# Program order, hand-dealt PSUM banks, one run of value products and idle products in an attention and mixer kernel

## The chip, the cores and the metric

The kernel runs on one core of a Trainium2 chip. The metric is the time of one execution in microseconds (us), median of several. Every number here is from a run of the original kernel ("before"), of the changed one ("after") or of one of twelve experiments. The kernel before scatters by about 1% from run to run, the changed ones by about 0.5%; a few runs of the kernel before counted as slow (883.67 us below is one) and are left out of every ratio.

## The reference

Two steps. First a thresholded attention over 8 batches, 8 heads, 576 positions and head size 64; of each row of scores only those within `tau` of the row's maximum are kept. Its output is then the input of a mixer: a low rank term over the positions and two dense layers.

```python
scores = scale * np.matmul(q, k.transpose(0, 1, 3, 2))
thresh = np.max(scores, axis=-1, keepdims=True) - tau
scores = np.where(scores >= thresh, scores, -1e9)
attn = np.exp(scores - max);  attn = attn / (sum + 1e-9)        # cut
x = np.matmul(attn, v)                                          # heads side by side: (8, 576, 512)
h = x.transpose(0, 2, 1) @ U @ V                                # rank 32
u = x + h.transpose(0, 2, 1)
out = u + np.maximum(u @ w_ch1, 0.0) @ w_ch2                    # 512 -> 2048 -> 512
```

## The kernel before

It goes through 32 pairs of heads (8 batches of 4), each in five row tiles: four of 128 rows, and a fifth with the last 64 rows of both heads. One step of the program is one row tile. Three pairs are in flight: the scores of pair p, the value products of p-1, and what follows them for p-2. The mixer of a finished batch is cut into units, put in beside the next batch's attention.

For a tile of scores, each head j uses its own half of the array's rows (partitions 0 to 63 or 64 to 127). VectorE then empties the PSUM and finds the row's extreme (`s_sb`), ScalarE exponentiates (`e_sb`), VectorE selects and sums (`w_ring`, `den`), and a DMA transposes the weights (`wT`).

```python
psS = pool("psS", 2, PSUM)      # two score tiles of two banks
ps1 = pool("ps1", 4, PSUM)      # four single banks for all else
...
sct = [psS.tile([P, 2, 512], FP32, name="sc", tag="sc") for _ in range(2)]
for c in range(2):
    for j in range(2):
        hs = slice(64 * j, 64 * j + 64)
        nc.tensor.matmul(sct[j][:, c, 0:HC], self.qT[hs, i * P:(i + 1) * P],
                         self.kT[hs, c * HC:(c + 1) * HC], start=True, stop=True)
```

In the fifth tile the second head's row sums lie in the other half of the partitions, so a tiny DMA moves them; the reciprocal of the sums reads it in the step in which the value products end:

```python
            if i == 4:
                if self.b % 2 == 0:
                    nc.sync.dma_start(self.den[0:HB, 4, 1:2], self.den[HB:P, 4, 0:1])
                ...                       # odd batches: two such copies
    def evacuate(self):                   # called at step 4 of the next pair
        ...
            nc.vector.tensor_scalar(out=self.rec[part, ts, :], in0=self.den[part, ts, :],
                                    scalar1=1e-9, scalar2=None, op0=ALU.add)
            nc.vector.reciprocal(out=self.rec[part, ts, :], in_=self.rec[part, ts, :])
```

The program states this order, but a scheduler of the framework decides the order in which each engine gets its instructions, and the pools decide which bank a tile gets. The scheduler takes this reciprocal early, almost a pair before its place in the program: in the stretch that the prediction shows, the copies were issued at 406.75 and 409.18 us, and VectorE stood at the reciprocal until 410.91.

## Time and profile before

| kernel before | |
|---|---|
| time, median of the first 3 runs | 874.38 us (867.46 to 883.67) |
| span of the profiled run | 869.7 us |
| mean granted TensorE clock | 0.931 (no record before 53.9 us; the views count that as 1.00) |
| start, until the first tile's end mark | 13.8 us |
| pairs 0 to 4, before the mixer has work | 106.7 us |
| 27 pairs with the mixer beside them | 690.8 us, 25.6 each |
| tail: the last batch's mixer | 58.4 us |

The stretches are cut at the last two transposes of a pair, the end of its attention weights. They are used the same way for each kernel below, so that "the middle" is always the same work: 27 pairs. The lines of the page, the stretches and the waits stand in the prediction. One line that it did not use belongs to the argument later. It is a row of the costliest groups: busy time, mean ns of one, then the engine's idle time just ahead of the group and what ended it.

```profile
L203 PE MATMUL sc<-qkT 64*128 64x288 f32 x1024 | 245.9, 477 | 21.6 <-DVE s_sb L219 21.1
```

These are the score products of the first four tiles, three tenths of all the time for which TensorE counts as busy (245.9 of 810.0 us).

### The profile page before, as it was taken

What the parts mean: (1) busy time and instruction counts of PE and PEld (TensorE: products, weight loads), DVE (VectorE), ACT (ScalarE), POOL (GpSimd) and SP (SyncE); (2) the same over time, 40 slices, a digit from 0 to 9 for tenths busy, and PEclk for the clock granted to TensorE, in tenths of its full rate; (3) what the DMA queues carried; (4) which work ended last, traced back from release to release, by engine and by line L of the source; (5) the groups of instructions that cost most, each with busy time, mean ns of one, the idle gap of its engine ahead of it and who ended that gap; (6) DMA issues with size and microseconds to landing.
All of it is one profiled execution on the core that took longest, in us unless ns stands there. A gap on an engine that the chain in (4) does not pass through costs nothing.

```text
span 869.7 us, 15087 instructions
## 1 busy us (share of the span) xinstructions
PE 810.0 (93%) x5064; PEld 458.3 (53%) x5064; DVE 532.1 (61%) x1548; ACT 446.8 (51%) x1089; POOL 310.7 (36%) x469
## 2 busy tenths in 40 slices
PE   5998899989999999989999999898999999999997
PEld 3554555534565556544566445553456545655473
DVE  3768686546766776456675577544676577746401
ACT  3545556624676447543476345653457644755260
POOL 9675655324443333243342444403443233000000
PEclk9998889968999999878899799996899999989989
DMA  6999988446654656444665478534567576424302
GB/s 124 149 163 169 154 140 117 86 86 119 129 103 81 123 123 112 84 99 84 108 109 96 106 120 125 103 50 103 118 105 98 87 119 129 82 46 73 69 1 61
DMA packets 225309, 90.29 MB, mean 104 GB/s; under 512 B 208512, under 2 KB 213568, under 8 KB 225232
## 3 DMA queue, kind: packets, MB, share of 16 engines
q1 hardware_dynamic: 205376, 56.98, 41.1%
q0 software_dynamic: 18640, 32.06, 18.7%
q8 instruction: 40, 0.66, 0.3%
q10 hardware_dynamic: 1216, 0.30, 0.2%
q14 instruction: 37, 0.30, 0.1%
HBM read 36.86 MB, written 9.44 MB: 53 GB/s over the span
## 4 chain that ended last, share of the span: by engine, by line
PE 56%; DVE 10%; DMA 9%; ACT 6%; SPq 5%; issue 2%; ACTq 0%; DVEq 0%
PE sc L203 13%; PE ch L370 13%; PE p L347 11%; DMA den<-den 9%; PE av L260 6%; DVE s_sb L219 5%; SPq L242 5%; ACT e_sb L226 5%; PE sc L211 4%; DVE w_ring L234 3%; PE ups L321 2%; PE qkps L146 2%; PE tps L311 2%; PE ch L373 1%; PE ups L323 1%
## 5 line engine op out<-in xcount | busy, mean ns | idle before, releaser
L226 ACT ACTIVATE e_sb<-s_sb,m 128x576 bf16<-128x576 f32 x288 | 216.1, 774 | 240.4 <-DVE s_sb L219 234.6
L219 DVE TENSOR_SCALAR_CACHE_REDUCE s_sb<-sc 128x576 f32<-128x576 f32 x288 | 209.5, 753 | 179.3 <-PE sc L203 143.9
L203 PE MATMUL sc<-qkT 64*128 64x288 f32 x1024 | 245.9, 477 | 21.6 <-DVE s_sb L219 21.1
L234 DVE SCALAR_TENSOR_TENSOR w_ring<-s_sb,thr,e_sb 128x576 bf16<-128x576 f32 x288 | 229.7, 820 | 38.0 <-ACT e_sb L226 29.1
L135 POOL TENSOR_TENSOR vh<-vraw,vh 128x512 bf16<-128x512 f32 x64 | 52.7, 841 | 397.9 <-ACT vh L134 355.0
L203 PEld LDWEIGHTS sc<-qkT 64*128 64x128 f32 x1024 | 129.1, 205 | 89.6 <-DVE s_sb L219 35.7
L347 PE MATMUL p<-uT,W1b 128*128 128x288 bf16 x1024 | 151.1, 295 | 5.6 <-ACT Rb L351 5.0
L370 PE MATMUL ch<-W2b,Rb 128*128 128x512 bf16 x512 | 134.8, 408 | 0.9 <-ACT uT L324 0.9
L260 PE MATMUL av<-wT,vh 128*64 128x288 bf16 (+1 forms) x1280 | 128.6, 310 | 1.4 <-DMA wT<-w_ring 1.3
L347 PEld LDWEIGHTS <-W1b 128*128 128x128 bf16 x1024 | 96.4, 100 | 60.9 <-issue 36.9
L260 PEld LDWEIGHTS <-vh 128*64 128x64 bf16 (+1 forms) x1280 | 76.7, 115 | 32.8 <-issue 19.3
L370 PEld LDWEIGHTS <-Rb 128*128 128x128 bf16 x512 | 49.0, 103 | 64.7 <-issue 24.2
L351 ACT ACTIVATE Rb<-p 128x288 bf16<-128x288 f32 x128 | 52.1, 407 | 23.9 <-PE p L347 23.5
L380 DVE TENSOR_TENSOR o<-ch,x 128x512 f32<-128x512 f32 x36 | 24.5, 680 | 61.5 <-PE ch L373 58.1
L355 ACT ACTIVATE Rb<-p 128x224 bf16<-128x224 f32 x128 | 45.9, 359 | 21.4 <-PE p L347 18.5
L211 PE MATMUL sc<-qkT 64*64 64x288 f32 x256 | 51.6, 453 | 0.5 <-DVE s_sb L219 0.5
L95 POOL DMA_DIRECT2D qraw<-in_q_dram x62 | 42.5, 686 | 23.5 <-PE qkps L146 22.5
L95 POOL DMA_DIRECT2D vraw<-in_v_dram x64 | 44.1, 690 | 12.4 <-POOL vh L135 6.2
L269 ACT COPY xT<-av 128x288 f32<-128x288 f32 x64 | 22.5, 402 | 49.4 <-PE av L260 39.4
L95 POOL DMA_DIRECT2D kraw<-in_k_dram x62 | 43.0, 694 | 9.3 <-PE qkps L146 8.8
L146 PE MATMUL qkps<-ident,kraw 128*128 128x128 f32 (+1 forms) x160 | 30.0, 298 | 15.1 <-ACT qkT L150 15.1
L96 POOL DMA_DIRECT2D vraw<-in_v_dram x64 | 41.1, 642 | 1.0 <-issue 0.6
(61 smaller groups left out, 674.2 us busy)
## 6 DMA issues: line engine op xcount, KB each, us to landing
out_dram<-o SPq DMA_DIRECT2D x72, 128.0 KB, 2.4
vraw<-in_v_dram POOLq DMA_DIRECT2D x64, 80.0 KB, 2.7
wT<-w_ring SPq DMA_TRANSPOSE x320, 3.4
qraw<-in_q_dram POOLq DMA_DIRECT2D x62, 80.0 KB, 3.4
kraw<-in_k_dram POOLq DMA_DIRECT2D x62, 80.0 KB, 4.0
vraw<-in_v_dram POOLq DMA_DIRECT2D x64, 64.0 KB, 2.9
qraw<-in_q_dram POOLq DMA_DIRECT2D x62, 64.0 KB, 3.4
kraw<-in_k_dram POOLq DMA_DIRECT2D x62, 64.0 KB, 4.1
```

Of the source, the lines that this page charges most:

```text
L95: engine.dma_start(raw[0:HB, :, j, :], sv[:, 0:NT, j, :])
L135: nc.gpsimd.tensor_tensor(out=vh[0:part, ts, 1, :, :], in0=src, in1=hi, op=ALU.subtract)
L146: nc.tensor.transpose(ps[:, n:n + rows(t)], raw[0:rows(t), t, :, :], ident[0:rows(t), 0:rows(t)])
L203: nc.tensor.matmul(sct[j][:, c, 0:HC], self.qT[hs, i * P:(i + 1) * P], self.kT[hs, c * HC:(c + 1) * HC], start=True, stop=True)
L211: nc.tensor.matmul(one[hs, c, 0:HC], self.qT[hs, 512:S], self.kT[hs, c * HC:(c + 1) * HC], start=True, stop=True)
L219: nc.vector.tensor_scalar(out=s_sb.rearrange("p (a c) -> p a c", a=2), in0=sct[x][:, :, 0:HC], scalar1=0.0, scalar2=None, op0=ALU.add, op1 ...
L226: nc.scalar.activation(out=e_sb, in_=ssb[x], func=ACT.Exp, bias=m[:, x:x + 1], scale=-1.0)
L234: nc.vector.scalar_tensor_tensor(out=w_sb[:, 0:S], in0=ssb[x], scalar=thr[:, x:x + 1], in1=esb[x], op0=ALU.is_le, op1=ALU.mult, accum_out= ...
L260: nc.tensor.matmul(self.av[c][64 * j:64 * j + 64, 0:HC], self.vh[0:nk, kt, part, j, :], self.wT[0:nk, kt, j, c * HC:(c + 1) * HC], start=( ...
L347: nc.tensor.matmul(ps[:, 0:HC], W1b[:, dt, ft * P:(ft + 1) * P], bt.uT[:, dt, c * HC:(c + 1) * HC], start=(dt == 0), stop=(dt == 3))
L351: nc.scalar.activation(out=bt.Rb[:, ft, 0:HC], in_=ps[:, 0:HC], func=ACT.Relu)
L370: nc.tensor.matmul(ch, lhsT, W2b[:, ft, :], start=(ft == 0), stop=False)
```

## The change

The intent: take the order of instructions out of the scheduler's hands, so that each engine finds its work in the order in which it becomes ready, and hand out the PSUM banks to match. Its core, cut:

```diff
-    psS = pool("psS", 2, PSUM)
-    ps1 = pool("ps1", 4, PSUM)
+    psum = pool("psum", 1, PSUM)
+    pair_bank = [psum.tile([P, 2, 512], FP32, name=f"scores{n}") for n in range(2)]
+    bank = [psum.tile([P, 512], FP32, name=f"bank{n}") for n in range(4)]
+    def bank1():                      # the bank that has been free longest
+        ...
-        nc.sync.dma_start(self.den[0:HB, 4, 1:2], self.den[HB:P, 4, 0:1])
+        nc.gpsimd.dma_start(self.den[0:HB, 4, 1:2], self.den[HB:P, 4, 0:1])
     def evacuate(self):
         ...
-            nc.vector.reciprocal(out=self.rec[part, ts, :], in_=self.rec[part, ts, :])
     def back(self):                   # now at step 3 of the next pair
+        nc.vector.tensor_scalar(out=self.rec, in0=self.den, scalar1=1e-9, ...)
+        nc.vector.reciprocal(out=self.rec, in_=self.rec)
     ...                               # mixer units
-        bt.Rb[:, ft, ...] relu of 288, or of 224 and 64
+        R2[:, ft, lo:lo + HC] relu of 288, two batches in one tile
-        for ft in (2 * g, 2 * g + 1):          # W2 products, 2 at a time
+        for ft in range(8 * g, 8 * g + 8):     # 8 at a time
     ...                               # the loop
+    order = ctx.enter_context(tc.manual_schedule())
+    fill(24)                                   # idle products, later 4 or 2 a step
+    share = (2.3, 1.4, 0.0, 2.3, 3.6)          # mixer work dealt to the five steps
     for i in range(NT):
         pair.scores(i)
+        if p < 6: fill(...)
-        if i in (2, 3): a.mm(2 * i - 4); a.mm(2 * i - 3)
-        elif i == 4: a.mm(4); a.evacuate()
+        if i == 2:                             # all 40 value products of a pair
+            for kt in range(NT): a.mm(kt)
+            late.append(a.evacuate)
     ...                               # output stores from sync to gpsimd; qkT, vhl, wT buffers 3 -> 2
```

## The prediction

> **What bounds the kernel now.** I read the page first (busy shares, clock row, chain), then the stretches between the last tiles of chosen head pairs, then the longest waits, then one stretch of the timeline in the middle. The kernel works on 32 head pairs (8 batches of 4), each in five row tiles; a batch's mixer (two dense layers) runs beside the next batch's attention. A pair's last tile shows as its two last transposes (line 242), so I cut the span there.
>
> ```profile
> PE 810.0 (93%) x5064; PEld 458.3 (53%) x5064; DVE 532.1 (61%) x1548; ACT 446.8 (51%) x1089; POOL 310.7 (36%) x469
> PEclk9998889968999999878899799996899999989989
> PE sc L203 13%; PE ch L370 13%; PE p L347 11%; DMA den<-den 9%; PE av L260 6%; DVE s_sb L219 5%; SPq L242 5%; ACT e_sb L226 5%; PE sc L211 4%; DVE w_ring L234 3%; PE ups L321 2%; PE qkps L146 2%; PE tps L311 2%; PE ch L373 1%; PE ups L323 1%
> ```
>
> TensorE looks full at 93%, VectorE has 39% spare; yet the chain goes for 9% through a copy of a few hundred bytes (den to den) and for 5% through the transposes queued ahead of it. In the stretches (columns: length, busy time and instructions of PE, PEld, DVE, ACT, POOL, then granted clock, DMA share, GB/s):
>
> ```profile
> 0.00:13.80 13.80, 5.01 (x18) 2.96 (x18) 0.38 (x9) 3.51 (x7) 12.51 (x24) 1.00 0.62 128
> 13.80:32.00 18.20, 16.90 (x52) 10.31 (x53) 14.88 (x45) 9.23 (x16) 15.03 (x24) 1.00 0.89 140
> 32.00:57.50 25.50, 25.38 (x102) 13.44 (x101) 15.27 (x47) 9.77 (x18) 18.67 (x31) 1.00 1.04 145
> 57.50:77.60 20.10, 17.49 (x103) 10.18 (x102) 15.12 (x48) 10.44 (x22) 12.56 (x19) 0.83 1.22 185
> ...
> 120.50:811.30 690.80, 655.57 (x4265) 369.75 (x4264) 446.81 (x1296) 372.78 (x922) 229.13 (x340) 0.93 0.57 100
> 811.30:869.70 58.40, 52.18 (x317) 29.53 (x314) 7.91 (x15) 18.56 (x60) 0.00 (x0) 0.94 0.17 39
> ```
>
> So: 13.8 us of start, 106.7 us for pairs 0 to 4 (no mixer yet), 690.8 us for 27 pairs with the mixer (25.6 us each), 58.4 us of tail. What breaks the middle is visible in the timeline:
>
> ```profile
> 409.69 0.86 PE L146 MATMUL qkps<-ident,kraw 128*128 128x128 f32 x5
> 410.91 0.17 DVE L273 TENSOR_SCALAR rec<-den 64x2 f32<-64x2 f32 x1 [1.06 <-DMA den<-den]
> 411.93 2.00 PE L203 MATMUL sc<-qkT 64*128 64x288 f32 x4 [1.39 <-DVE s_sb L219]
> 415.87 3.48 PE L370 MATMUL ch<-W2b,Rb 128*128 128x512 bf16 x8
> 422.34 1.90 PE L370 MATMUL ch<-W2b,Rb 128*128 128x512 bf16 x8
> ```
>
> VectorE takes its work in order. It sits at the reciprocal of the row sums until the tiny DMA lands; the next scores wait for VectorE to empty their PSUM; TensorE goes idle for 1.4 us, and the eight W2 products that then follow take 3.48 us, where six us later they take 1.90. One wait costs itself and several us at half clock. The list of waits puts it at 27 times:
>
> ```profile
> DVE rec L273 <- DMA den<-den: 45.1, 27, 5.2
> PE sc L203 <- DVE s_sb L219: 21.1, 20, 3.1
> ```
>
> **What the Trainium skill says.** "TensorE: Matmul & The Clock Gate", Part 1, says that the array runs at half rate by default and after about 3.4 us of too little activity, and at full rate after a busy window of that length. The trace agrees on the factor (3.48 against 1.90 us). It also shows the cold start: the page's clock row says 1.00 up to 57 us, but a score tile there takes 2.29 us against 1.17 later, so I trust durations over that row. "Perfetto Trace Analysis", Identifying the Most-Contended Engine, calls matmul busy time a bad measure of headroom; here the 93% contain half-clock matmuls, so it agrees. "PSUM — Partial Sum Buffer", Specifications: eight banks of 512 fp32 per partition. Two score tiles of two banks leave four, as many as the after kernel deals out by hand. "DMA: Bandwidth & Descriptors", SWDGE vs HWDGE: a GpSimd-issued DMA starts later (about 1 us against 0.6). No run shows that yet; den copies and stores move there.
>
> **The change part by part.**
> Removed from the path: the den wait. The copy goes out on GpSimd's queue, and the reciprocal moves to step 3 (of 5) of the next pair, over 12 us later; landing here takes 2 to 5 us. 45 us of VectorE waiting go, and with it most of the 97 us at half clock in the middle (0.93 granted means 14% of 690.8 us at half, so 48 us lost).
> Removed outright: each mixer unit empties PSUM with one 288-wide relu (407 ns) where every second unit had two (359 + 225 ns): 128 x 0.18 us = 23 us of ScalarE, which isn't the bound. The separate reciprocals for tile 4 go too, about 32 x 0.35 us of VectorE.
> Added: 98 idle products of 128x512 before and in the first six pairs. At 0.216 us (16 such took 3.45 us in the tail) they are 21 us of TensorE, some 4 us a pair in a stage where TensorE has room.
> Moved: all 40 value products in one run at step 2; mixer work dealt to steps by a credit of 2.3, 1.4, 0, 2.3 and 3.6.
>
> TensorE's work for one middle pair at full clock, from start-to-start gaps in undisturbed stretches: scores 4 x 1.17 + 1.12 = 5.8; values 40 x 74 ns (24 took 1.78) = 3.0; q and k transposes 1.58; x transposes 0.65; turn 1.23; low rank 0.5; mixer (128 x 129 ns + 9 x 1.83 + 4.5 x 0.31 = 34.3 a batch)/4 = 8.6. Sum 21.4 us. Checked against before: 25.6 less 1.8 (clock, 48/27) less 1.3 (35 us without a matmul, /27) is 22.5, so about 1.1 us of small bubbles stay inside the busy time.
> VectorE for one pair: nine tiles of 0.68 + 0.75 us, five thresholds of about 0.28, 1.6 for row scaling and reciprocal, 0.8 for output sums: 16.6 us. It never binds over a pair. Step by step TensorE needs about 4.5, 4.2, 4.2, 4.2, 5.2 us, VectorE 3.2, 3.9, 3.9, 4.7, 2. Scores of the next tile only need the previous tile's two evacuations (1.5 us after the scores end), and TensorE has 3 us of other work in between. So in the middle TensorE should run without gaps and keep its clock. An even batch has less mixer work (34 credits of 38), so about two steps a batch run dry and lose perhaps 3 us: 0.4 to 0.8 a pair. I take 22.6 us a pair: 27 x 22.6 = 610 us (before 691).
> Start: the first transposes came at 8.4 us after the loads, cold. The 24 idle products end about there, the transposes and first scores then run warm: 13 us (before 13.8).
> Pairs 0 to 4: VectorE's order binds. Pair 0: 4 x 3.3 + 2.3 = 15.5. Pairs 1 to 4: 3.3, 3.3, 4.6 (values in one run), 4.5, 2.3 = 18, and 1 us for late transposes: 19 each, 76 together. 92 us (before 106.7).
> Tail: 58.4 us, mostly 128 + 80 mixer products, unchanged. Slightly less cold: 56.5 us.
> Sum: 13 + 92 + 610 + 56.5 = 771.5 us of span, and 2 us from span to time (871.55 against 869.7): 773 us.
>
> **The rivals.**
> DMA takes over in pairs 1 to 4. For: the two queues' shares add up to 1.02 to 1.24 there, since the mixer's weights load meanwhile, and a transpose lands in 6.0 us (median) against 3.2 in the middle; the value run at step 2 waits for the last transposes, issued about 8 us before, and in a fixed order nothing overtakes it. Against: TensorE waited on transposes only 1.3 us in this stage. It would cost 3 to 4 us a pair: 785 us.
> Fixed order turns each lateness into a stall. For: the scheduler could fill a gap with mixer work, here a relu behind a waiting exponential holds a bank (four in all), and the next product waits. Against: relu takes 0.41 us per 0.52 us of products, ScalarE is used for 14 of 22 us. Costs 1 to 2 us a pair: 800 to 825 us.
> The clock isn't kept: where the mixer's queue is dry, TensorE idles up to 3 us in a step and halves. Three or four us a batch: 795 us.
> The opposite: bubbles vanish and 21.4 us hold: 740 us.
> Stores and den copies behind 12 load issues of 0.66 us on GpSimd could hold an output buffer (three); sums are about 4 us apart, so I expect little.
>
> **Range and chances.** All but one rival lie above the sum, all below 830, because the half clock and the den wait do disappear. 745 to 815 us should hold it 8 times in 10. Faster by over 2% (below 857) 0.95, within 2% 0.04, slower 0.01.
>
> **What would show it.** Right: no den in the chain of waits; granted clock over 0.97 in the middle; pairs 22 to 23 us apart by their last transposes; score tiles at 1.17 us and clock kept from the first pair on; tail within 3 us of 58. Wrong: value products waiting on transposes for over 1 us a pair in the first 110 us (DMA); TensorE waiting on relus (banks); scores waiting on VectorE by over 20 us in total; a clock near 0.93 still; first stage over 110 us.

## The result

The changed kernel took 754.44 us (median of 4 runs, 751.19 to 755.76), beside 873.4 for the kernel before on the same chip: a ratio of 0.8652, 95% interval 0.8595 to 0.8709. Ratios here are the mean time of one kernel's fast runs over that of the other's of the same rounds, so not quite the ratio of the quoted medians. The output was correct.

The page of the changed kernel, the same three lines that the prediction shows of before (busy time, granted clock, chain of waits):

```profile
PE 710.8 (95%) x5119; PEld 422.0 (56%) x5162; DVE 523.3 (70%) x1489; ACT 434.7 (58%) x961; POOL 380.2 (51%) x589
PEclk9998799999999999999999999999999999999998
PE bank L437 16%; PE scores L250 16%; PE bank L415 16%; PE bank L315 10%; DVE s_sb L267 5%; PE scores L258 4%; DVE w_ring L289 4%; PE bank L214 3%; ACT e_sb L275 3%; PE bank L390 2%; DMA wT<-w_ring 2%; PE bank L375 2%; PE bank L474 1%; PE bank L441 1%; PE bank L392 1%
```

TensorE's busy share rose by two points only, although 99 us of busy time are gone: the share says little, the sum much. The chain no longer holds a den copy, nor the transposes in SyncE's queue, and products of TensorE make up most of it. After the first slices the clock row reads 9, that is 90% or more, up to the last one.

The stretches (length, then busy time and instructions of PE, PEld, DVE, ACT and POOL, then granted clock, DMA share and GB/s): start, pairs 0 to 4 one by one, the middle, the tail.

```profile
0.00:11.30 11.30, 9.64 (x43) 4.61 (x44) 0.67 (x13) 3.51 (x7) 10.30 (x21) 1.00 0.64 136
...
45.40:63.70 18.30, 16.41 (x117) 9.63 (x118) 15.80 (x46) 10.88 (x22) 14.18 (x22) 0.97 1.15 166
63.70:91.00 27.30, 19.83 (x113) 10.91 (x113) 15.15 (x45) 10.78 (x22) 14.14 (x22) 0.75 1.23 173
91.00:110.20 19.20, 17.06 (x121) 9.99 (x122) 15.35 (x46) 10.89 (x22) 12.87 (x19) 0.94 1.18 173
110.20:692.00 581.80, 570.70 (x4248) 343.75 (x4277) 439.06 (x1244) 363.60 (x812) 293.30 (x450) 1.00 0.70 121
692.00:749.40 57.40, 47.67 (x303) 27.25 (x304) 6.72 (x12) 16.39 (x41) 9.42 (x18) 0.96 0.18 40
```

| stretch | before | predicted | after |
|---|---|---|---|
| start | 13.8 | 13 | 11.3 |
| pairs 0 to 4 | 106.7 | 92 | 98.9 |
| 27 pairs with the mixer | 690.8 (25.6 each) | 610 (22.6 each) | 581.8 (21.55 each) |
| tail | 58.4 | 56.5 | 57.4 |
| sum | 869.7 | 771.5 | 749.4 |

So 109 of the 120 us come from the middle, and two terms of the sum are off: the middle was 28 us better than predicted, pairs 0 to 4 seven worse. The seven are one pair: the fourth took 27.3 us at a clock of 0.75, and its neighbours 18 and 19. The timeline shows a part of it (start, length, what ran, how often, and in brackets the idle time ahead with what ended it):

```profile
71.98 0.31 PE L315 MATMUL bank<-wT,vh 128*64 128x288 bf16 x2
76.46 0.42 PE L315 MATMUL bank<-wT,vh 128*64 128x288 bf16 x1 [4.17 <-DMA wT<-w_ring]
78.31 4.85 PE L315 MATMUL bank<-wT,vh 128*64 128x288 bf16 x37 [1.43 <-DMA wT<-w_ring]
```

The run of value products waits 5.6 us for the attention weights' transposes, the granted clock falls to half (recorded from 76.2 to 83.0 us), and the 37 products that follow take 4.85 us, where 40 of them take 2.76 in the middle. While they wait the mixer's weights are being loaded: the DMA share of that stretch is 1.23. But the clock was at half once before in this pair, from 62.5 to 69.3 us, ahead of any wait for transposes.

What did a pair in the middle gain? A stretch of TensorE there, after:

```profile
396.88 1.24 PE L250 MATMUL scores<-qkT 64*128 64x288 f32 x8
398.05 2.76 PE L315 MATMUL bank<-wT,vh 128*64 128x288 bf16 x40
400.74 1.24 PE L250 MATMUL scores<-qkT 64*128 64x288 f32 x8
```

And two of before. Each of a tile's four products is two records, so x8 is a whole tile of scores:

```profile
330.90 0.75 PE L203 MATMUL sc<-qkT 64*128 64x288 f32 x2
332.20 1.14 PE L347 MATMUL p<-uT,W1b 128*128 128x288 bf16 x8 [0.55 <-ACT Rb L351]
333.27 1.23 PE L203 MATMUL sc<-qkT 64*128 64x288 f32 x6
```

After, a tile of scores goes through whole: from its start to the next start are 1.17 us. Before, the scheduler puts mixer products after the first product of the tile, and one product alone (x2) takes 0.7 us, the other three about 1.15. "TensorE: Matmul & The Clock Gate", Part 3 (Packing small matmuls), in the Trainium skill says that products on different row groups of the array run at the same time. The two heads of a tile are on different halves of the rows, and the trace agrees: in the whole tile at 396.88 us the two heads' records start in pairs, 6 to 7 ns apart, and alone, one product takes over half as long as all four together. A cut tile therefore costs more than a whole one with the same products. This was not in the prediction.

### The profile page after: what moved, and what is told of

It reads as the page before. It is cut to its first block, busy times and chain, and to the rows that moved or that the text cites. A ratio compares the mean times of both kernels' runs of the same rounds, so it can differ in the third digit from the quotient of the medians.

```text
span 749.4 us, 15084 instructions
## 1 busy us (share of the span) xinstructions
PE 710.8 (95%) x5119; PEld 422.0 (56%) x5162; DVE 523.3 (70%) x1489; ACT 434.7 (58%) x961; POOL 380.2 (51%) x589
## 4 chain that ended last, share of the span: by engine, by line
PE 77%; DVE 10%; ACT 5%; issue 3%; DMA 3%; POOL 1%; DVEq 0%; SPq 0%; POOLq 0%; ACTq 0%
PE bank L437 16%; PE scores L250 16%; PE bank L415 16%; PE bank L315 10%; DVE s_sb L267 5%; PE scores L258 4%; DVE w_ring L289 4%; PE bank L214 3%; ACT e_sb L275 3%; PE bank L390 2%; DMA wT<-w_ring 2%; PE bank L375 2%; PE bank L474 1%; PE bank L441 1%; PE bank L392 1%
## 5 line engine op out<-in xcount | busy, mean ns | idle before, releaser
L267 DVE TENSOR_SCALAR_CACHE_REDUCE s_sb<-scores 128x576 f32<-128x576 f32 x288 | 208.3, 748 | 103.8 <-PE scores L250 99.3
L250 PE MATMUL scores<-qkT 64*128 64x288 f32 x1024 | 167.7, 433 | 7.9 <-DVE s_sb L267 7.4
L415 PE MATMUL bank<-uT,W1b 128*128 128x288 bf16 x1024 | 145.8, 286 | 7.3 <-ACT R L421 6.8
L437 PE MATMUL bank<-W2b,R 128*128 128x512 bf16 x544 | 131.4, 380 | 3.4 <-issue 2.5
L250 PEld LDWEIGHTS scores<-qkT 64*128 64x128 f32 x1024 | 93.5, 187 | 53.4 <-issue 16.3
L415 PEld LDWEIGHTS <-W1b 128*128 128x128 bf16 x1024 | 94.0, 97 | 47.5 <-issue 21.4
L421 ACT ACTIVATE R<-bank 128x288 bf16<-128x288 f32 x256 | 97.3, 409 | 6.9 <-PE bank L415 1.4
L315 PE MATMUL bank<-wT,vh 128*64 128x288 bf16 (+1 forms) x1280 | 91.4, 292 | 5.8 <-DMA wT<-w_ring 5.6
L437 PEld LDWEIGHTS <-R 128*128 128x128 bf16 x576 | 51.7, 98 | 66.0 <-issue 12.0
L450 DVE TENSOR_TENSOR o<-bank,x 128x512 f32<-128x512 f32 x36 | 24.8, 690 | 37.1 <-issue 21.2
L123 POOL DMA_DIRECT2D kraw<-in_k_dram x62 | 43.9, 708 | 1.3 <-DMA W1b<-in_moe_w_ch_dram 0.8
L124 POOL DMA_DIRECT2D kraw<-in_k_dram x62 | 40.9, 660 | 2.4 <-DMA W1b<-in_moe_w_ch_dram 2.4
```

The lines of the kernel that those rows point to most:

```text
L123: engine.dma_start(raw[0:HB, :, j, :], sv[:, 0:NT, j, :])
L124: engine.dma_start(raw[HB:P, 0:4, j, :], sv[:, NT:9, j, :])
L267: nc.vector.tensor_scalar(out=s_sb.rearrange("p (a c) -> p a c", a=2), in0=self.sct[x][:, :, 0:HC], scalar1=0.0, scalar2=None, op0=ALU.add ...
L315: nc.tensor.matmul(self.av[c][64 * j:64 * j + 64, 0:HC], self.vh[0:nk, kt, part, j, :], self.wT[0:nk, kt, j, c * HC:(c + 1) * HC], start=( ...
L415: nc.tensor.matmul(ps[:, 0:HC], W1b[:, dt, ft * P:(ft + 1) * P], bt.uT[:, dt, c * HC:(c + 1) * HC], start=(dt == 0), stop=(dt == 3))
L421: nc.scalar.activation(out=R2[:, ft, lo:lo + HC], in_=ps[:, 0:HC], func=ACT.Relu)
```

## The experiments

Two questions: how much of the middle is the den wait, as the prediction had it; and what makes the rest. Theories: (A) the wait and the half clock after it are nearly all; (B) the order of the program is; and, formed after the first results, (S) score tiles that stay whole.

### The den wait alone, in the kernel before

```diff
-                    nc.sync.dma_start(self.den[0:HB, 4, 1:2], ...)      # and the other two
+                    nc.gpsimd.dma_start(self.den[0:HB, 4, 1:2], ...)
     def evacuate(self): ...
-        (the eight lines that make self.rec)
     def back(self): ...
+        (the same eight lines)
```

> The kernel before with one part of the change: the copies of the row sums go out on GpSimd's queue, and the reciprocals are taken only when the pair is transposed back, a whole pair later. The scheduler still orders everything. Theory A (the wait of VectorE for this copy, and the half clock after it, is most of the loss in the middle): the 45 us of VectorE waiting go and most of the 97 us at half clock, so 785 to 815 us, pairs in the middle about 23 us apart. Theory B (the fixed, packed order is what counts, the wait was only one symptom): 840 to 865 us, with the clock still at 0.93 to 0.95 in the middle.

Measured: 819.92 us (817.53 to 822.67), ratio 0.9387 (0.9344 to 0.9429): between the two ranges, nearer to A's. The middle, and what is left of the wait (us in total, times, longest):

```profile
116.40:758.00 641.60, 624.29 (x4240) 358.00 (x4269) 447.97 (x1297) 371.95 (x923) 260.92 (x394) 0.98 0.64 110
...
DVE rec L279 <- DMA den<-den: 10.5, 8, 1.6
```

The middle is 49 us shorter than before, and 60 longer than after. The clock went from 0.93 to 0.98. As an estimate, a granted share c of a stretch loses (1-c) of it, 48 us before and 13 here; TensorE's idle time fell from 35 to 17 us. The two sum to 53 us: the mechanism is the predicted one, but it is less than half of the middle's gain. The wait is not quite gone, 10.5 us of VectorE's 45.1 are left, since the scheduler still takes some reciprocals early; TensorE waits only 3.9 us for evacuated scores in this middle (13.5 before). Its longest wait there, which the prediction passes over, is that of the q and k transposes for ScalarE's copies: 15.1 us before, 9.8 here, none that the list names in after.

### Program order alone, in the kernel before

```diff
+    ctx.enter_context(tc.manual_schedule())
     pairs[0].load(nc.sync, nc.scalar)
```

> The kernel before with nothing changed but that each engine runs its instructions in the order in which the program gives them. In that order the reciprocal comes a pair after its copy, so the wait is gone too. Theory A: about as the run with the wait taken out, 785 to 820 us. Theory B in its strong form (any fixed order does): 750 to 780 us. Theory C (a fixed order pays only when evacuations and banks are placed by hand): 830 to 900 us, with TensorE waiting on copies behind one another.

Measured: 913.45 us (909.90 to 915.52), ratio 1.0441 (1.0399 to 1.0484): slower. The program of before is not written to be taken literally. TensorE now stands behind work that is not ready:

```profile
PE tps L311 <- ACT qkT L150: 29.3, 23, 2.3
PE p L347 <- ACT Rb L351: 17.1, 14, 1.2
```

(Two of the three longest waits of TensorE.) VectorE's wait for the den copy is gone here. A fixed order alone does not pay; the waits point to evacuations that stand too late in it.

### The den wait put back into the changed kernel

```diff
-        (in back(): tensor_scalar and reciprocal that make self.rec)
+    def recip(self):
+        (the same)
     ...
+            if i == 4 and pair:
+                pair.recip()          # at the end of its own pair
```

> The changed kernel with the wait put back: the reciprocal stands at the end of its own pair, right after the copies are issued, so VectorE must wait for them. Theory A: VectorE stands 3 to 6 us per pair, the next scores wait, TensorE idles 1 to 3 us and its clock halves at least in some pairs: 800 to 850 us. Theory B: TensorE has 3 to 4 us of other work queued at that point, the wait is mostly covered: 755 to 785 us with the clock above 0.97.

Measured: 812.01 us (808.15 to 813.36), ratio 0.9279 (0.9241 to 0.9316), 58 us more than after. The copies are still on GpSimd's queue; only the place of the reciprocal differs. The waits of VectorE and what they do to TensorE:

```profile
DVE rec L329 <- DMA d_ring<-d_ring: 125.2, 32, 6.1
PE scores L250 <- DVE s_sb L267: 47.5, 21, 6.0
```

VectorE stands at the reciprocal in each of the 32 pairs. This fits A for the size of the wait (55 us off in one kernel, 58 on in the other; in the middle alone 49 and 43), and it shows that the place of the reciprocal matters: another queue alone would not have removed the wait. The other half, a later reciprocal with the copies left on SyncE's queue, was not tried.

### The changed kernel with the scheduler's order

```diff
-    order = ctx.enter_context(tc.manual_schedule())
```

> The changed kernel in all but the fixed order: the scheduler is given the same program, with the same PSUM tiles named by hand, and orders each engine itself. Theory B (the order by hand is what the other half of the gain is): as far above the changed kernel as the run with only the wait taken out, 805 to 850 us. Rival (the hand-placed banks, the single relu and the values in one run are what count, whoever orders): 750 to 775 us.

Measured: 760.25 us (756.57 to 762.63), ratio 0.8711 (0.8655 to 0.8766). The middle, and VectorE's wait:

```profile
113.06:702.94 589.88, 579.24 (x4242) 346.73 (x4272) 438.64 (x1244) 362.68 (x812) 286.82 (x448) 1.00 0.68 120
...
DVE rec L335 <- DMA d_ring<-d_ring: 29.3, 17, 3.3
```

Only 6 us are lost, and the two ratios' intervals overlap, so theory B falls: the order need not be fixed. That is less than to say that order does not matter. Compared place by place the two orders on TensorE differ in over two thousand of 5,119, but mostly by shifts; all but some 270 instructions stand in the same sequence. What makes the middle short was handed to the scheduler with the program and its banks. The run also shows that a den wait need not cost anything: VectorE stood 29.3 us at the reciprocal again, 17 times, and TensorE was idle for no longer than in after (10.6 and 11.1 us in the middle).

### Value products in two steps

```diff
         elif i == 2 and a:
-            for kt in range(NT): a.mm(kt)
-            late.append(a.evacuate)
+            for kt in range(3): a.mm(kt)
+        if i == 3 and a: a.mm(3); a.mm(4); early.append(a.evacuate)
         (back, narrow, low_rank and turn each one step later)
```

> The changed kernel with the value products of a pair split over two steps (24 and 16 of 40), the transposes back a step later, low rank and turn a step later. If a single run of values saves time by itself (TensorE's gaps at each change of kind): 4 to 15 us slower, 758 to 770 us. If only the order without waits counts: 750 to 758 us.

Measured: 780.26 us (778.59 to 784.11), ratio 0.8950 (0.8895 to 0.9005), a miss for both: 26 us more than after. But this does not measure the split alone. From start to next start the two parts take 1.61 and 1.24 us, together 0.16 us more than the 2.69 of one run, 4 us over 27 pairs. The rest goes with what I had to move along with it: TensorE's idle time in the middle doubled from 11 to 24 us. Which of the moves did it stays open.

### Idle products left out

```diff
-        for _ in range(n):
+        for _ in range(0):
             nc.tensor.matmul(ps, idle[:, 0:P], idle, start=True, stop=True)
```

> The changed kernel without the 98 idle products. If they matter as the prediction has it: the first transposes and pairs 0 to 4 run at half clock at least in part (score tiles at 2.3 us), the start is 1 to 2.5 us longer, pairs 0 to 4 some 5 to 15 us longer; 760 to 770 us. Rival: VectorE's order binds these pairs anyway and the idle products cost what they gain: 750 to 757 us.

Measured: 761.25 us (753.91 to 762.04), ratio 0.8686 (0.8638 to 0.8735), overlapping the interval of after. In its profile, of the fastest of its runs (a span of 752.1 us), the start takes 13.5 us instead of 11.3, and pair 4 ends at 114.6 instead of 110.2. That is the predicted kind of gain, of some 4 us; the runs allow anything from 0 to 7, so it is under 1% and not settled. The changed kernel's first stretch shows what the idle products do:

```profile
1.19 6.96 PE L474 MATMUL bank<-idle 128*128 128x512 bf16 x24 [1.19 <-DVE idle L63]
...
10.05 1.24 PE L250 MATMUL scores<-qkT 64*128 64x288 f32 x8 [0.47 <-ACT qkT L226]
```

The first tile of scores takes 1.24 us; before, the first one took 2.29.

### Whole score tiles in the kernel before

The first experiment's trace still had 40 pieces of one product (x2) between 140 and 685 us, that is tiles cut after their first product or before their last; the trace of after had none. The obvious way to forbid the cut is to make the two heads' tiles one. This goes on top of the first experiment:

```diff
-                sct = [psS.tile([P, 2, 512], FP32, ...) for _ in range(2)]
+                four = psS.tile([P, 2, 2, 512], FP32, ...)
+                sct = [four[:, x, :, :] for x in range(2)]
-    psS = pool("psS", 2, PSUM)
+    psS = pool("psS", 1, PSUM)
```

> The kernel before with the wait taken out (as the first run) and, besides, the two score tiles of a step held as one PSUM tile of four banks, so that the scheduler can't start a step's first product when only one half is free. The traces suggest theory S: a score tile whose four products run together takes 1.17 us, since two products side by side use the two halves of the array's rows; the scheduler cut about half of the tiles into one product and three (0.69 and 1.11 us), and that is most of what the run with the wait taken out still lacks. S: no tile is cut, 770 to 795 us. Rival (placing of values, relus and banks by hand makes the difference): 808 to 830 us, since the evacuations now gate a whole step.

Measured: 809.65 us (807.33 to 814.00), ratio 0.9251 (0.9173 to 0.9329). The total is in the rival's range. But the stretches tell two things apart (pairs 0 to 4, then the middle):

```profile
13.80:132.10 118.30, 85.59 (x506) 49.70 (x508) 79.40 (x232) 53.31 (x109) 67.63 (x103) 0.78 0.91 139
132.10:751.30 619.20, 593.90 (x4203) 340.90 (x4234) 447.58 (x1297) 369.15 (x913) 257.46 (x388) 0.99 0.63 113
```

The middle is 22 us shorter than in the first experiment, with 20 pieces of one product where there were 40; the scheduler cut others in the middle instead (36 pieces of two products, 18 there). Pairs 0 to 4 are 16 us longer (102.6 there), at much the same clock (0.78 and 0.80). In these pairs TensorE waits 14.7 us for evacuated scores (5.0 there) and 17.7 for transposes of the weights (9.5 there). The first would follow from a single four-bank tile, in which no score product may start before both evacuations are done; I did not test that.

### Score tiles cut in the changed kernel

The sharper test is the other way round: everything as in after, with one unit of mixer work between the first product of a tile and the other three.

```diff
                 for c in range(2):
                     for j in range(2):
+                        if c == 0 and j == 1:
+                            between()              # mix(1)
                         nc.tensor.matmul(sct[j][:, c, 0:HC], ...)
```

> The changed kernel with one mixer unit moved between the first product of a score tile and the other three, wherever the dealt credit allows; same work, fixed order. Theory S: each cut costs 0.6 to 0.7 us of TensorE, with 60 to 100 cuts 40 to 65 us: 790 to 820 us. Rival (a cut costs only the change between kinds, under 0.1 us): 754 to 765 us.

Measured: 809.36 us (806.93 to 811.23), ratio 0.9237 (0.9176 to 0.9298), in S's range. The timeline, the middle, and the row of the score products here and, last, in after:

```profile
405.23 0.75 PE L252 MATMUL scores<-qkT 64*128 64x288 f32 x2
405.91 0.67 PE L417 MATMUL bank<-uT,W1b 128*128 128x288 bf16 x4
406.51 1.24 PE L252 MATMUL scores<-qkT 64*128 64x288 f32 x6
...
113.40:749.30 635.90, 622.53 (x4238) 358.75 (x4265) 434.21 (x1237) 364.22 (x808) 287.61 (x448) 1.00 0.59 110
...
L252 PE MATMUL scores<-qkT 64*128 64x288 f32 x1024 | 222.2, 437 | 12.3 <-DVE s_sb L269 11.8
...
L250 PE MATMUL scores<-qkT 64*128 64x288 f32 x1024 | 167.7, 433 | 7.9 <-DVE s_sb L267 7.4
```

The cut tile takes 0.68 and 1.16 us from start to next start, 0.67 more than a whole one (1.17). The same products that were busy 167.7 us in after are busy 222.2 here, close to the 245.9 of before. The clock is 0.989: this loss has nothing to do with it. TensorE's idle time in the middle is 13 us (11 in after), so a rival by way of the banks, that the moved mixer unit makes TensorE wait, has little room.

Does one measure fit all of these? I took the score products of the first four tiles between 140 and 685 us of each trace, the time from each group's start to the next start on TensorE (at most its own length), and divided by its records (each trace taken as one piece). A middle has 27 x 4 x 8 = 864 such records.

| kernel | pieces of one product | ns per record | difference x 864, an estimate | middle, measured | difference, measured |
|---|---|---|---|---|---|
| after | 0 | 150.3 | | 581.8 | |
| after, scheduler's order | 10 | 162.6 | +11 us | 589.9 | +8 us |
| after, tiles cut | 60 | 209.2 | +51 us | 635.9 | +54 us |
| before, den wait off | 40 | 196.1 | | 641.6 | |
| the same, whole tile | 20 | 165.8 | -26 us | 619.2 | -22 us |

Three differences of middles are accounted for by the score products to within 4 us. Between after and "before, den wait off" the same working gives (196.1 - 150.3) x 864 = 40 of the 60 us.

### The weights' loads: none, or fewer at a time

First the wrong kernel (relative error 2.85), to see what the loads of the mixer's weights cost in all; then W2's eight loads in every second step.

```diff
-            nc.gpsimd.dma_start(W1b[:, t, cs], moe_w_ch1[...])          # and W2b likewise
+            nc.gpsimd.memset(W1b[:, t, cs], 0.01)
```

> The changed kernel with the mixer's weights filled with a constant instead of loaded (wrong result on purpose). If DMA binds in pairs 1 to 4, as my first rival has it: no wait of value products on transposes there, pairs 1 to 4 take 17 to 18.5 us each instead of 20.5, and the time falls by 6 to 12 us, to 742 to 748 us. If VectorE's order binds them: within 2 us of the changed kernel.

Measured: 749.52 us (748.01 to 749.66), ratio 0.8587 (0.8540 to 0.8635), about 5 us less than after and between the two expectations. TensorE did not wait for transposes in the fourth pair, so the loads are behind that wait. Yet the pair still took 24.4 us, part of it at half clock. That does not clear the loads of the rest, for the fill has a cost of its own, as the fourth pair shows:

```profile
72.16 5.24 DVE L280 TENSOR_SCALAR thr<-m 128x2 f32<-128x2 f32 x1
...
74.62 2.75 POOL L149 MEMSET W2b<- 128x1024 bf16 x3
```

A threshold instruction of VectorE (median 0.17 us) took 5.24 us and ended with a run of three memsets on GpSimd. Two more small VectorE instructions went the same way, at 56.53 us (2.52 us long) and at 98.19 us (3.42), each until three memsets were done. So this run does not tell what the loads cost in all.

```diff
-            if p >= 1 and loadq:
+            if p >= 1 and loadq and (len(loadq) > 8 or i % 2 == 0):
                 loadq.pop(0)()
```

> The changed kernel with the eight loads of the second weight spread over every other step, up to where they are needed, instead of one a step. Correct result. If the crowding of DMA in pairs 3 and 4 costs: 3 to 8 us less than the changed kernel, 746 to 752 us, and no wait of several us for transposes in pair 3. If not: 753 to 757 us.

Measured: 752.56 us (748.98 to 755.36), ratio 0.8628 (0.8580 to 0.8677): no gain that can be told from none. The fourth pair kept a wait of 7.2 us. W1's loads fall on it, and these I had left as they were.

### The same loads spread over more pairs

So W1's loads were spread too, over pairs 1 to 3, with the small loads before them in pair 0 and W2's after them in pairs 4 and 5:

```diff
-            if p >= 1 and loadq:
+            g = 5 * p + i
+            if g in (3, 4) or g in range(5, 20, 2) or g in range(21, 29):
                 loadq.pop(0)()
```

On the same chip ran the changed kernel unaltered once more, as a yardstick:

> The changed kernel unaltered, for a comparison on the same chip with the run that follows: 751 to 757 us.

> The changed kernel with both weights' loads moved: the small ones from pair 0, the first weight's eight loads on every other step of pairs 1 to 3, the second's in pairs 4 and 5, where no more than the middle's DMA load lies beside them. Correct result. If crowded DMA is what holds pairs 1 to 4 (the constant weights gave 748 to 750 us): 5 us less than the changed kernel, 747 to 751 us, and no wait of several us of value products on transposes before pair 5. If the wait only moves to another pair: within 2 us of it.

Measured: 753.40 us for the changed kernel (750.74 to 753.96, 6 runs, ratio 0.8645, 0.8611 to 0.8679), 746.61 with the loads spread (742.91 to 750.67, 6 runs, ratio 0.8576, 0.8519 to 0.8634), with a correct result. That is the fastest correct kernel, 6.8 us or 0.9% below after by the medians. The intervals of the two ratios overlap, but they share the scatter of the kernel before; side by side, all six runs of the one lie below all six of the other. The fourth pair, and the wait in the whole run:

```profile
64.56:84.43 19.87, 17.78 (x124) 10.38 (x124) 16.10 (x48) 11.09 (x23) 11.90 (x19) 0.94 1.16 165
...
PE bank L315 <- DMA wT<-w_ring: 2.2, 3, 1.2
```

19.9 us instead of 27.3, at a clock of 0.94 instead of 0.75; the waits for transposes fell from 5.6 us, the longest 4.2, to 2.2, the longest 1.2. So the timing of the weights' loads makes this pair long or short. Which of the three shifts did it was not separated, and the half clock early in the pair is shorter here (63.4 to 66.8 us) but not gone. "DMA: Bandwidth & Descriptors", Issuing engines are not separate DMA queues, says that DMAs of all issuing engines end up on the same 16 DMA engines and interleave there; this agrees, since the loads are issued by GpSimd and the transposes by SyncE.

## Why the prediction was right or wrong

Its time, 773 us, is 18.6 us or 2.5% above the measured 754.44, and the measurement lies in its range of 745 to 815. "Faster" was right. By its steps:

1. **"Removed from the path: the den wait."** Right, in both directions: without it the kernel before gains 55 us, with it the changed one loses 58. But the prediction let the wait and the clock account for nearly all of the gain in the middle. Alone they gave 49 of 109 us there. Nor does VectorE's wait cost by itself: with the scheduler's order in the changed kernel it stood 29.3 us for the copy, at no visible cost.
2. **"I take 22.6 us a pair".** This is the mis-sized term: measured 21.55, so 28 us over 27 pairs. The bare sum of TensorE's work, 21.4 us, was right. What failed is the working around it: "so about 1.1 us of small bubbles stay inside the busy time". They were no bubbles. The sum had put in 1.17 us for every tile of scores, as read "from start-to-start gaps in undisturbed stretches", and the disturbed ones, tiles cut by mixer products, were left over as a remainder. The per-record measure puts their cost at (196.1 - 150.3) x 32 records = 1.5 us a pair in the kernel before without the den wait, somewhat more than that remainder. I carried it over to the changed kernel in part, and there it vanishes: all 101 tiles in the counted stretch went through whole.
3. **"about two steps a batch run dry and lose perhaps 3 us: 0.4 to 0.8 a pair".** Not seen: TensorE is idle for 11.1 us in all of the middle, 0.4 us a pair for every reason together (6.8 us of it waits for relus), and the clock is 1.00.
4. **Pairs 0 to 4: "92 us".** Too low by 7 us. The rival "DMA takes over in pairs 1 to 4" was right in kind: the run of value products waits for late transposes. But it is not 3 to 4 us in each pair; it is one pair, 5.6 us of waiting and two stretches of half clock, one of them before the wait. Spreading the loads removes most of it.
5. **Start, "13 us", and tail, "56.5 us".** 11.3 and 57.4. The first tile of scores is warm, as predicted; idle products and transposes ended earlier than I had taken. What the 98 idle products are worth in total time is within the scatter. The "some 4 us a pair" for them is a slip: 74 of the 98 fall in six pairs, 16 us or 2.7 a pair.
6. **Rival "Fixed order turns each lateness into a stall", 800 to 825 us.** Wrong for this program: TensorE waits 6.8 us for relus and 7.4 us for evacuations of scores in the whole run. It is right in kind for the other one: the old program in fixed order took 913 us.
7. **Rival "bubbles vanish and 21.4 us hold: 740 us".** This is what happened in the middle; the late transposes in pair 3 made up part of the difference.
8. **What would show it.** Den gone from the chain, clock over 0.97 in the middle, tail within 3 us, scores waiting on VectorE for less than 20 us: all seen. "pairs 22 to 23 us apart" was too long. Of the signs that it would be wrong, one came up, barely: value products waited for transposes for 5.6 us in the first 110 us, 1.1 us a pair, though all of it in one pair. "first stage over 110 us" did not, at 98.9. "score tiles at 1.17 us and clock kept from the first pair on" held only to 62.5 us: the clock was at half for 17 us in all between there and 93.2.
9. **Small slips.** The timeline has 3.62 us for a run of 16 W2 products, not 3.45, and the step-by-step needs sum to 22.3 us for TensorE and 17.7 for VectorE, not to the 21.4 and 16.6 of the lines above them. None of these moves the result.

Where the middle's 109 us come from, then: 49 from the den wait and the half clock it caused (run alone). The other 60 can be read from the two timelines, summed from start to next start over the whole middles. The score products of the first four tiles take 167.0 us in the kernel before without the den wait and 128.8 in after: 38 us. W2 products take 9.9 us less (4.8 of it half clock), W1 products 3.1 less, TensorE's gaps 4.8 less. Value products take 10.9 us less, but the scores of the fifth tile, with which the scheduler had mixed them, 7.5 more: 3 us together. The half clock left in the first of the two costs 12 us by this count, and these are spread over the items named, only 2 of them in the score products. So the one run of 40 value products is worth some 3 to 4 us (the split lost 4 in these products). What the one-piece relus do was not taken apart.

Why the scheduler cuts fewer tiles in the changed program (10 pieces of one product against 40) is not shown by any run either.

## What to carry to other kernels

When products that run at the same time on two halves of the array belong together, keep them adjacent on TensorE: look in the timeline for groups that are broken up, and sum a kernel's work from all groups, not from the undisturbed ones; what remains as "bubbles" may be just those. A small DMA whose result an in-order engine reads should be read one stage later; here another queue with an early reader did not help (812 us), and a scheduler may move the reader forward again, so look for it in the trace. After a change that lets TensorE run without gaps, look at the start: loads that nobody noticed before may now hold up the first transfers on which the products wait.

## What the Trainium skill lacked or had wrong

- "TensorE: Matmul & The Clock Gate", Part 3, gives the gain of packed row groups, and nothing of what it costs when another product comes between them. Here a tile of four fp32 products on two row halves took 1.17 us whole, and 0.68 + 1.16 us cut after the first, 0.67 us more; in a kernel with 60 such cuts between 140 and 685 us the total rose by 55 us.
- The same page, Part 1, agrees on the factor of two. It puts the fall to half rate after an idle window of about 3.4 us; here no gap of that length was needed. In the stretch of before that the prediction shows, a gap of 1.39 us, with q and k transposes ahead of it, was enough: the record falls to half at 412.3 us, and the eight W2 products soon after took 3.48 us instead of 1.90. In all 14 recorded falls of before, the longest gap of TensorE in the 3.4 us ahead was between 1.0 and 2.8 us.
- No page says that a trace may hold no clock record at first. In before the first one, a rise to full, comes at 53.9 us (in after at 4.5). The views count the time ahead of it as 1.00, though the first tile of scores there takes 2.29 us, against 1.17 to 1.24 at full rate; so the mean of 0.931 is too high.
- "DMA: Bandwidth & Descriptors" has no figure for what DMA transposes suffer beside bulk loads. Here the run of value products waited 5.6 us for them in one pair beside the weights' loads, at a DMA share of 1.23, and 2.2 us in all when the loads were spread.
- No page says what a tiny copy between partitions costs where other transfers are under way and an in-order reader stands right behind it: 125.2 us over 32 pairs, up to 6.1 us at a time, in the run with the reciprocal put back.
